# Turning chunks on the partitions in a gated-attention and MoE kernel, with a list scheduler's due times by stage

## The chip, the cores and the metric

The kernel runs on one core of a Trainium2 chip. The metric is the device time of one execution in microseconds (us). Before the change it was 332.19 us, the median of three runs (331.95 to 332.5). The engines are written as in the profile: PE (TensorE, matrix products; PEld its weight loads), DVE (VectorE), ACT (ScalarE), POOL (GpSimd), and SP (SyncE, which only issues transfers here). "SPq" in a chain of waits is time in which SP's queue is issuing a transfer. The core has 16 DMA engines.

## The reference

A linear attention with complex decay, whose output goes through a gated two-layer network:

```python
mag = np.sqrt(a_re * a_re + a_im * a_im)
scale = np.minimum(mag, 0.999) / (mag + 1e-06)
# a_re_n, a_im_n = a_re * scale, a_im * scale
for t in range(S):                      # B=4, H=8, S=768, D=48
    new_re = ar * S_re - ai * S_im
    new_im = ar * S_im + ai * S_re
    kv = np.einsum('bhd,bhe->bhde', k[:, :, t], v[:, :, t])
    S_re, S_im = (new_re + kv, new_im)
    y[:, :, t] = np.einsum('bhd,bhde->bhe', q[:, :, t], S_re)
# x = y as [3072, 384]
gate = 1.0 / (1.0 + np.exp(-(x @ w_gate)))
val = x @ w_val
return (gate * val @ w_out)             # w_gate, w_val [384, 1536], w_out [1536, 384]
```

All inputs and the output are float32. q, k, v, a_re and a_im have the shape (batch 4, heads 8, tokens 768, 48).

## The kernel before

The tokens of a batch are cut into six chunks of 128, one token on each SBUF partition: 24 chunks in all. The recurrence inside a chunk becomes products with triangular masks: cumulative sums over tokens of the log magnitude (`cl`) and of the phase (`ct`). A planner (a list scheduler that runs when the program is built) decides in which order each engine gets its instructions, from costs, buffers and "due times".

Each load takes one tensor of one chunk, 128 tokens x 8 heads x 48 numbers. A head's 48 numbers are 192 contiguous bytes in DRAM, so one load is 1024 pieces of 192 bytes:

```python
def dma_in(dst, src, b, c):
    nc.sync.dma_start(
        heads(dst), src[b, :, c * L:(c + 1) * L].rearrange("h t d -> t h d"))
```

A chunk has five of them: a_re, a_im (step `la`), then k, q, v (step `lq`). The phase of a chunk must start from the sum over all earlier chunks of the batch. Before, POOL keeps a running sum `run` of whole tiles and PE adds its column sums with a second product, against a matrix `on_t` of equal entries:

```python
nc.tensor.matmul(ct, wt_t, T[A][:, 1, s], start=True, stop=False, ...)
if prev:
    nc.tensor.matmul(ct, on_t, T[prev[0]], start=False, stop=False, ...)
# ... cut ...
nc.gpsimd.tensor_tensor(out=T[RUN], in0=T[prev[0]], in1=th, op=ALU.add)
```

After that `ct` is rounded on DVE (`r16`), the rounded turns are taken off by a small product (`nid_t`), and ACT makes sine and cosine.

## Time and profile before

| | before |
|---|---|
| time, median | 332.19 us |
| span of the profiled execution | 328.5 us |
| busiest engine | PE, 262.5 us (80%) |
| hardware DMA queue | 148,368 packets, 51.2% of 16 engines' span |
| first squares on ACT / first gate product on PE | 14.45 us / 44.12 us |

The lines themselves stand in the prediction. The groups there read: line, engine, operation, output<-inputs, shapes, count | busy us, mean ns of one | idle time before them and what ended it. The page's slices cut the span in 40; a digit is a busy share in tenths.

### The profile page before, as it was taken

The page shows a single profiled execution, that of the slowest core. Times are in us where ns is not written, and L with a number is a line of the kernel's source. Part 1 is how long each engine was busy: PE and PEld are TensorE (multiplying, and loading weights), DVE is VectorE, ACT ScalarE, POOL GpSimd, SP SyncE. Part 2 cuts the span into 40 slices and gives each one's busy share as a digit, 9 for nine tenths or more (in the row PEclk, how much of TensorE's full clock was granted, in tenths as well). Part 3 has the DMA queues.
Part 4 walks back from the last instruction along what each step waited for, and adds up shares of the span by engine and source line. Part 5 has one row for each costly group of instructions (what it writes and reads, how often), then busy time and mean ns, then how long its engine had stood idle before and what let it go on. Part 6 is the DMA issues. An engine that isn't in the chain of part 4 may idle for free.

```text
span 328.5 us, 6196 instructions
## 1 busy us (share of the span) xinstructions
PE 262.5 (80%) x2256; PEld 169.7 (52%) x2256; DVE 206.5 (63%) x373; ACT 211.9 (65%) x354; POOL 166.1 (51%) x177
## 2 busy tenths in 40 slices
PE   0035685857978799898969989989999898999995
PEld 0012552535545455465646555656666565666564
DVE  2002930399699679287755696689567949891522
ACT  0356438666877987896389848867995358543433
POOL 0187275867997877687117961945485104000000
PEclk9997757799999999999998999999999999999999
DMA  6998995997999588581886048736120011002011
GB/s 124 188 182 128 189 178 85 138 196 108 160 123 218 76 129 160 123 145 11 148 166 113 1 82 154 153 54 118 50 26 2 0 50 28 0 2 73 2 48 48
DMA packets 152381, 32.68 MB, mean 99 GB/s; under 512 B 144904, under 2 KB 152352, under 8 KB 152352
## 3 DMA queue, kind: packets, MB, share of 16 engines
q1 hardware_dynamic: 148368, 28.76, 51.2%
q0 software_dynamic: 3984, 3.54, 7.6%
q8 instruction: 17, 0.28, 0.4%
q14 instruction: 12, 0.10, 0.1%
HBM read 31.07 MB, written 4.76 MB: 109 GB/s over the span
## 4 chain that ended last, share of the span: by engine, by line
PE 42%; ACT 20%; DVE 18%; issue 8%; SPq 4%; DMA 4%; POOL 3%; DVEq 0%; ACTq 0%; POOLq 0%
PE o L717 12%; PE g L679 8%; PE v L679 7%; PE cl L389 5%; ACT L769 5%; DVE qkT L556 4%; DVE p L701 3%; DVE qst L518 3%; DVE kst L518 3%; SPq L309 3%; PE ct L463 2%; ACT g L694 2%; ACT sq L333 2%; ACT a L449 2%; POOL lm L342 2%
## 5 line engine op out<-in xcount | busy, mean ns | idle before, releaser
L694 ACT ACTIVATE g<-g 128x384 f16<-128x384 f32 (+2 forms) x108 | 48.2, 456 | 55.4 <-PE g L679 53.5
L701 DVE SCALAR_TENSOR_TENSOR p<-g,v 128x384 f16<-128x384 f16 (+2 forms) x108 | 53.7, 504 | 23.2 <-PE v L679 15.7
L679 PE MATMUL g<-xt,wg 128*128 128x384 f16 (+2 forms) x324 | 65.5, 312 | 3.0 <-DVE xt L662 1.5
L679 PE MATMUL v<-xt,wv 128*128 128x384 f16 (+2 forms) x324 | 65.5, 312 | 0.9 <-DVE p L701 0.9
L717 PE MATMUL o<-wo,p 128*128 128x384 f16 x288 | 52.0, 326 | 0.0
L389 PE MATMUL cl<-lm,wl_t 128*128 128x384 f32 x48 | 22.7, 607 | 27.8 <-ACT lm L365 24.9
L441 POOL TENSOR_TENSOR qk<-qk,ee 128x768 f32<-128x768 f32 x24 | 43.3, 1813 | 2.0 <-ACT ee L398 2.0
L490 DVE TENSOR_SCALAR r<-ct 128x384 f16<-128x384 f32 x24 | 13.2, 552 | 43.9 <-PE ct L463 25.9
L679 PEld LDWEIGHTS <-wg 128*128 128x128 f16 x324 | 29.5, 99 | 20.5 <-issue 8.0
L679 PEld LDWEIGHTS <-wv 128*128 128x128 f16 x324 | 28.7, 99 | 17.0 <-issue 5.8
L518 DVE TENSOR_TENSOR kst<-qk,cs 128x768 f16<-128x768 f32 x24 | 26.1, 1089 | 17.6 <-ACT cs L509 17.5
L556 DVE COPY qkT<-tp 128x1024 f16<-128x1024 f16 x48 | 32.6, 683 | 6.9 <-PE tp L549 6.6
L598 POOL CAST x<-u 128x384 f16<-128x384 f32 x20 | 14.1, 707 | 44.4 <-DVE u L588 38.4
L717 PEld LDWEIGHTS <-p 128*128 128x128 f16 x288 | 27.1, 98 | 18.2 <-issue 2.1
L571 DVE TENSOR_TENSOR mst<-sc,msk_t 128x512 f16<-128x512 f32 x48 | 32.6, 684 | 5.5 <-PE sc L564 5.4
L342 POOL TENSOR_TENSOR lm<-sq 128x384 f32<-128x384 f32 x24 | 28.1, 1170 | 13.7 <-ACT sq L333 12.3
L769 ACT ACT_TABLE_LOAD x27 | 34.6, 1283 | 0.5
L382 POOL TENSOR_TENSOR a<-a 128x384 f32<-128x384 f32 x24 | 23.6, 1008 | 22.0 <-ACT a L371 19.5
L463 PE MATMUL ct<-a,wt_t 128*128 128x384 f32 x48 | 22.1, 544 | 8.9 <-ACT a L449 8.9
L549 PE MATMUL tp<-idn_t,qst 128*128 128x128 f16 x192 | 26.5, 221 | 3.2 <-DVE qst L518 3.2
L389 PEld LDWEIGHTS cl<-lm,wl_t 128*128 128x128 f32 x48 | 10.4, 235 | 34.9 <-ACT lm L365 28.9
L548 PE MATMUL tp<-idn_t,kst 128*128 128x128 f16 x192 | 27.0, 221 | 0.8 <-DVE P L618 0.4
(52 smaller groups left out, 462.6 us busy)
## 6 DMA issues: line engine op xcount, KB each, us to landing
a<-in_a_re_dram SPq DMA_DIRECT2D x24, 192.0 KB, 3.9
a<-in_a_im_dram SPq DMA_DIRECT2D x24, 192.0 KB
qk<-in_k_dram SPq DMA_DIRECT2D x24, 192.0 KB, 4.9
qk<-in_q_dram SPq DMA_DIRECT2D x24, 192.0 KB, 4.8
v<-in_v_dram SPq DMA_DIRECT2D x24, 192.0 KB, 4.1
out_dram<-ot SPq DMA_DIRECT2D x24, 192.0 KB, 1.9
wg<-in_moe_w_gate_dram POOLq DMA_DIRECT2D x3, 384.0 KB, 5.7
wv<-in_moe_w_val_dram POOLq DMA_DIRECT2D x3, 384.0 KB, 6.4
```

Of the source, the lines that this page charges most:

```text
L342: nc.gpsimd.tensor_tensor(out=T[LM][:, s], in0=T[SQ][:, 0, s], in1=T[SQ][:, 1, s], op=ALU.add)
L389: nc.tensor.matmul(T[CL][:, :HD], wl_t, T[LM][:, s], start=True, stop=True)
L441: nc.gpsimd.tensor_tensor(out=T[QK], in0=T[QK], in1=T[EE], op=ALU.mult)
L463: nc.tensor.matmul(ct, wt_t, T[A][:, 1, s], start=True, stop=False, skip_group_check=True)
L518: nc.vector.tensor_tensor(out=T[SL][i].rearrange("p h (r x) -> p h r x", r=2)[:, :, :, 0:D], in0=heads(T[QK][:, i]).unsqueeze(2) .broadcas ...
L556: nc.vector.tensor_copy(out=T[QT], in_=T[TP])
L571: nc.vector.tensor_tensor(out=T[MS], in0=T[SC], in1=msk_t.unsqueeze(1).broadcast_to([L, 4, L]), op=ALU.mult)
L679: nc.tensor.matmul(T[ACC][:, :nt], w[:, j, fb * 128:fb * 128 + 128], T[XT][:, j, :nt], start=(j == 0), stop=(j == 2))
L694: nc.scalar.activation(out=T[G16][:, :nt], in_=T[PG][:, :nt], func=FT.Tanh, scale=0.5)
L701: nc.vector.scalar_tensor_tensor(out=T[PT][:, fb, :nt], in0=T[G16][:, :nt], scalar=1.0, op0=ALU.add, in1=T[PV][:, :nt], op1=ALU.mult)
L717: nc.tensor.matmul(T[PO][:, :DM], T[PT][:, fb, s * L:(s + 1) * L], wo16[:, fb], start=(fb == 0), stop=(fb == NFB - 1))
L769: nc.scalar.preload_act_table_set(SETS[held])
```

## The change

The intent is to do without the second phase product and the running sum in batches 1 to 3. Chunk c is laid on the partitions turned by c tokens, so its last token lies on the partition where the next chunk has its first token. The carry then is one row, which DVE adds in place in a 32-row window; the masks turn with the chunk. The due times become a table by stage and group, the first group is one chunk whose elementwise work DVE does, and table loads of ACT are placed explicitly. The planner now also sorts its candidates (`sorted(ready, key=self.rank.get)`), where the planner before walks a Python set. The core of the diff:

```diff
-SIZES = [2, 3, 3, 3, 3, 3, 3, 3, 1]
-RATE = 9.21
-LEAD = {'la': 87.6, 'lq': -0.9, 'p0': 39.8, 'pa': 40.0, 'pb': 17.2}
+ROLL = 1
+BRISK = 1
+SIZES = [1, 2, 2, 2, 3, 3, 3, 3, 3, 2]
+DUE = {
+    "la": [-88.8, 5.9, -62.3, -45.2, -110.2, -63.1, -93.9, 4.9, 23.3, 64.9],
+    # ... cut: 17 more stages ...
+}
 # ... cut ...
+    tok = (np.arange(L)[None] + np.arange(NCH)[:, None]) % L
+    upto = tok[:, :, None] <= tok[:, None, :]
+    last = (tok == L - 1).T * TWO_PI
 # ... cut ...
+    def turn(b, c):
+        return c if b >= ROLL else 0
+
+    def pieces(b, c):
+        r = turn(b, c)
+        return [(slice(0, L - r), slice(c * L + r, (c + 1) * L))] + (
+            [(slice(L - r, L), slice(c * L, c * L + r))] if r else [])
+
     def dma_in(dst, src, b, c):
-        nc.sync.dma_start(
-            heads(dst), src[b, :, c * L:(c + 1) * L].rearrange("h t d -> t h d"))
+        for p, t in pieces(b, c):
+            nc.sync.dma_start(
+                heads(dst[p]), src[b, :, t].rearrange("h t d -> t h d"))
 # ... cut ...
+    END = slice(L - 32, L)
 # ... cut ...
-            if c < NCH - 1:
+            if c < NCH - 1 and not rolled:
                 RUN = t_run(m)
 # ... cut ...
+            if rolled and c < NCH - 1 and s < n - 1:
+                def e(T, CT=CT, A=A, s=s, c=c):
+                    nc.vector.scalar_tensor_tensor(
+                        out=T[A][END, 1, s + 1], in0=T[CT][END, :HD],
+                        scalar=lst_t[END, c:c + 1], op0=ALU.mult,
+                        in1=T[A][END, 1, s + 1], op1=ALU.add)
```

The output stores are cut by the same `pieces`.

## The prediction

> **What bounds the kernel now.** I read the page from the top: busy shares, the forty slices, the DMA queues, the chain that ended last.
>
> ```profile
> span 328.5 us, 6196 instructions
> ...
> PE 262.5 (80%) x2256; PEld 169.7 (52%) x2256; DVE 206.5 (63%) x373; ACT 211.9 (65%) x354; POOL 166.1 (51%) x177
> ...
> PE   0035685857978799898969989989999898999995
> ...
> DMA  6998995997999588581886048736120011002011
> ...
> q1 hardware_dynamic: 148368, 28.76, 51.2%
> ...
> PE 42%; ACT 20%; DVE 18%; issue 8%; SPq 4%; DMA 4%; POOL 3%; DVEq 0%; ACTq 0%; POOLq 0%
> ```
>
> See three things. TensorE is the bound from about 140 us on (tenths of 9), and it is mostly idle in the first 60 us. The chain runs through PE, ACT and DVE; transfers are only 4% of it. And yet the transfers are not cheap: hardware queue q1 keeps 51.2% of 16 engines' span busy, and the first 70% of the slices stand at 5 to 9 tenths, because 120 loads (24 chunks x a_re, a_im, k, q, v) move in pieces of 192 bytes. They are hidden because they come early and because 16 DMA engines share each of them.
>
> So I measured the price of one piece, from the DMA view of two stretches in which loads ran without a gap, 95.8 to 101.2 us and 13 to 20 us:
>
> ```profile
> q1 hardware_dynamic: 5494, 1.09, 131.3%
> ```
>
> ```profile
> q1 hardware_dynamic: 6923, 1.31, 142.4%
> ```
>
> 5.4 us x 16 engines / 5494 packets = 15.7 ns; 7 us x 16 / 6923 = 16.2 ns. (The shares exceed 100% because a packet's record overlaps its neighbour's; the elapsed time counts.) One engine therefore takes about 16 ns per 192-byte piece. A load of 128 rows x 8 heads is 1024 pieces, 64 per engine, 1.0 us on 16 engines. Output rows of 1536 bytes, from the DMA view of the last 28.5 us (932 packets, 12.2%): 0.122 x 16 x 28.5 / 932 = 60 ns each.
>
> **What the Trainium skill says.** "DMA: Bandwidth & Descriptors", section "Why a DMA increments its semaphore by 16 and not by 1", says how many engines a DMA runs on: the largest k up to 16 that divides the slowest dimension of both access patterns; "127 partitions or a `[1, 1]` scalar → 1", and on the hardware path the lowest-numbered k. Every tile of the kernel before that is loaded from q, k, v and a has 128 rows, k = 16, which its 1.0 us agrees with; no trace here shows 127 rows yet. The same page, "Queues, rings and completion order", says that each engine consumes its ring in order, so a full-width load behind a narrow one waits on the shared engine. "Rules for kernel authors" there asks for an outermost size that is a multiple of 16.
>
> **The change part by part.**
>
> *On the core, gains.* 15 of the 20 carried chunks lose the second phase product (two passes each; these rows are from the groups by line):
>
> ```profile
> L466 PE MATMUL ct<-run,on_t 128*128 128x384 f32 x40 | 17.0, 507 | 0.0
> L479 POOL TENSOR_TENSOR run<-run,a 128x384 f32<-128x384 f32 x16 | 16.7, 1041 | 8.5 <-ACT a L449 5.0 <-PE ct L466 2.3 <-DMA v<-in_v_dram 0.9
> L769 ACT ACT_TABLE_LOAD x27 | 34.6, 1283 | 0.5
> ```
>
> PE: 30 x 0.507 = 15.2 us at that mean (12.8 us as a share of the row's 17.0 busy). POOL: 12 running sums x 1.04 + 3 copies x 0.51 = 14.0 us. ACT: 33 table loads in the trace, 30 in the new program: 3.8 us. DVE gains 21 carry operations on 32 rows (9 fused, 6 products, 6 sums), some 0.55 us each as the rounding of the same 384 columns costs: +11.6 us, in series with ct, rounding and next ct. A first group of one chunk, its elementwise work on DVE, starts on two loads alone. Before, the first squares wait until 13.15 us for four loads and the first gate product starts at 44.1; summing the chain's durations for one chunk I get about 6 us for the load and 20 us of work, so 26 to 28 us. More groups (10 for 9) move the same 110,592 columns of gate and value work. Together perhaps 25 to 35 us less: **about 300 us, if loads stay hidden.**
>
> *On the queue, the cost.* Turning chunk c of batches 1 to 3 by c rows splits every load into 128-c rows and c rows. By the rule: 127 rows 1 engine, 126 on 14, 125 on 5, 124 on 4, 123 on 3. Engine 0 serves all of them. Its pieces per load, big part plus small: c=0 64; c=1 1016+1; c=2 72+8; c=3 200+8; c=4 248+8; c=5 328+8: sum 1961, where an unturned batch gives it 384. One load of 127 rows takes 1016 x 16 ns = 16.3 us instead of 1.0, and a chunk has five.
>
> The program order (SP queue 189 rows before, 295 now) places the loads of chunks 0 to 6 first, almost as before: 35 loads, at least 36 us on all engines. I put the first 127-row load at 50 us. Then:
>
> - loads from there on, counted in the program: 29,095 pieces on engine 0 x 16 ns = 465.5 us;
> - output rows on the same engine before the last loads (k rule again): 466 x 60 ns = 28 us;
> - waits in which the in-order queue has nothing in flight: eight decay round trips after their scratch writes at 2 us, and about 10 us where the last q, k, v loads stand behind chunk 15's output, which waits for the phase work of the last group: 25 us;
> - after the last load: multiplies with the phase, attention of chunks 22 and 23, two thirds of group 8's gate work, group 9's, the outputs: before, 43 us passed from chunk 23's phase product (285.4) to the end with four chunks' output work left; about 37 us.
>
> 50 + 465 + 28 + 25 + 37 = 605 us span; measured time stood 3.7 us above the profiled span before (332.2 against 328.5), so about 609.
>
> What lies beside what: all gains on PE, POOL and ACT fall into time in which these engines now wait for loads. A chunk costs engine 0 on average 1961 x 5 x 16 ns / 6 = 26 us, against 11.7 us per chunk of the kernel before (281 us from the first gate product at 44 to 325, 24 chunks). Buffers can't hide it: it is throughput, not latency.
>
> **The rivals.**
>
> 1. *The engine rule doesn't bite* (the hardware spreads 127 rows after all). Then the core's gains stand: about 300 us. For it: the due times are plainly tuned, which suggests a planner that saw a gain. Against it: that planner charges 2.3 and 3.45 us a chunk whatever its rows, so it can't see the rule.
> 2. *SP issue becomes the bound*: 106 more DMAs at 0.4 to 1.0 us (issue records of the timeline) = 40 to 100 us more of queue time, 200 to 260 in all, still under the span; alone it would give 300 to 340 us.
> 3. *The serial carry*: cy, ct 1.3, rounding 0.56, correction 0.3, cy 0.55: 2.7 us x 15 = 40 us if wholly exposed, against 15 removed. Alone 310 to 340 us, inside the noise of the answer.
> 4. *A single engine runs quicker by itself* than beside 15 others: at 13 ns per piece the sum falls by 87 us to 520; at 18 ns (the queue's 51.2% x 16 x 328.5 / 148368) it rises by 58 to 668.
>
> **Range and chances.** Rivals 4 and my 50, 25 and 37 us give 520 to 690 about 610. Rival 1 I hold at about one in ten. So faster by over 2%: 0.09, within 2%: 0.02, slower: 0.89.
>
> **What would show it.** Right: loads of a turned chunk take 16 us or more from issue to landing where they took 4 to 5; the DMA row of the slices drops to about a tenth (one of 16 engines) from 50 us on while packets stay near 150,000 and q1's share falls to some 28%; PE below 50% busy, its clock often granted low; DMA and SPq lead the chain; ACT's squares and POOL's q, k products wait for DMA. Wrong: loads still land in 4 to 5 us and PE stays above 80%. The head is right if the first gate product starts near 27 us; the carry is right if its operations last about 0.55 us and nothing waits long for them. Mis-sized: the pieces' 16 ns, read off a stretch with one engine busy.

## The result, and the profile after

The changed kernel takes 537.81 us (median of 4 runs, 533.9 to 538.21); the kernel before, beside it on the same chip, 332.07 us (330.98 to 332.5). The ratio is 1.6178, 95% interval 1.6106 to 1.625: slower. Ratios in this document are the mean time of one kernel's fast runs over that of the other's of the same rounds, so not quite the ratio of the quoted medians.

The page of the changed kernel, in the same order as before:

```profile
span 532.1 us, 6426 instructions
...
PE 274.6 (52%) x2298; PEld 183.0 (34%) x2298; DVE 228.7 (43%) x410; ACT 210.3 (40%) x368; POOL 146.4 (28%) x158
...
PE   1467602304776068200277609700355779799973
...
DMA  9999403005432250000543261000243220122011
GB/s 158 190 195 186 66 16 55 18 16 120 95 55 61 52 105 18 17 16 16 128 66 65 61 113 22 16 17 16 51 78 82 55 45 1 36 63 58 28 46 30
...
q1 hardware_dynamic: 149741, 29.75, 27.9%
...
SPq 61%; PE 13%; DMA 12%; issue 5%; ACT 3%; DVE 3%; POOL 1%; ACTq 0%; POOLq 0%; DVEq 0%
...
L532 POOL TENSOR_SCALAR v<-v 128x384 f16<-128x384 f32 x24 | 14.3, 594 | 210.8 <-DMA v<-in_v_dram 206.6
```

The packets are almost as many as before, but q1's share fell from 51.2% to 27.9%. The GB/s row shows why: long stretches at 16 to 18, others at about 65 and 55. In those slices or just after them PE goes to 0. The kernel before moves mostly 80 to 200 in its first 28 slices:

```profile
GB/s 124 188 182 128 189 178 85 138 196 108 160 123 218 76 129 160 123 145 11 148 166 113 1 82 154 153 54 118 50 26 2 0 50 28 0 2 73 2 48 48
```

The chain is 61% SP's issues, and POOL's conversion of v alone waits 206.6 us for loads.

A turned chunk's loads in SP's timeline (start, duration, queue, line, output<-input, transfers joined in the row), chunk with one turned row first, then the next chunk's:

```profile
205.40 12.02 SPq L390 DMA_DIRECT2D a<-in_a_im_dram  x2
217.52 12.05 SPq L390 DMA_DIRECT2D qk<-in_k_dram  x2
229.62 11.98 SPq L390 DMA_DIRECT2D qk<-in_q_dram  x2
241.64 12.07 SPq L390 DMA_DIRECT2D v<-in_v_dram  x2
253.76 0.95 SPq L390 DMA_DIRECT2D a<-in_a_re_dram  x2
```

Each x2 is one split load. The load of 127 + 1 rows holds SP's queue for 12.0 us, the load of 126 + 2 rows for 0.95 us. An uncut load held it 1.0 us in the kernel before, where loads ran without a gap. The records behind the joined rows show where the time lies: the issue of the 127 rows takes 0.2 to 0.4 us, and the issue behind it, that of the single row, stands for 11.2 to 14.2 us. No semaphore that this second issue waits for changes in that time. So SP is neither busy computing addresses nor waiting for data: the second issue stands until the 127 rows are nearly through (they land about 1.6 us after it ends). The next view, the DMA view of the changed kernel from 206 to 240 us, in 40 parts, says how many engines are at work:

```profile
GB/s 16 16 16 16 16 16 16 16 16 16 16 16 36 16 18 12 16 16 16 16 16 16 16 16 16 16 16 16 18 16 16 16 16 16 16 16 16 16 16 16
```

And the same view from 285 to 300 us, where loads of 124 and then of 123 rows run:

```profile
GB/s 65 66 61 65 66 66 66 65 65 66 60 62 66 66 66 65 66 66 59 40 49 49 49 49 49 49 49 51 55 47 49 92 49 49 49 49 49 49 57 261
```

16, 49 and 65 GB/s are 1, 3 and 4 times 16.3: one engine for 127 rows, three for 123, four for 124. The completion semaphores in the trace agree. A load of 128 rows raises its semaphore in 16 updates, a load of 127 rows in 2: one 0.4 to 0.7 us after its issue, the other 13.5 to 16.2 us after it, when the data has landed. Loads of 126, 125, 124 and 123 rows make 15, 6, 5 and 4 updates, one more than the 14, 5, 4 and 3 engines.

The gain that was foretold for the head is there: the first gate product starts at 26.58 us (44.12 before).

### The profile page after: what moved, and what is told of

Same layout as the page of the kernel before. It is cut to its first block, busy times and chain, and to the rows that moved or that the text cites. A ratio compares the mean times of both kernels' runs of the same rounds, so it can differ in the third digit from the quotient of the medians.

```text
span 532.1 us, 6426 instructions
## 1 busy us (share of the span) xinstructions
PE 274.6 (52%) x2298; PEld 183.0 (34%) x2298; DVE 228.7 (43%) x410; ACT 210.3 (40%) x368; POOL 146.4 (28%) x158
## 3 DMA queue, kind: packets, MB, share of 16 engines
q1 hardware_dynamic: 149741, 29.75, 27.9%
## 4 chain that ended last, share of the span: by engine, by line
SPq 61%; PE 13%; DMA 12%; issue 5%; ACT 3%; DVE 3%; POOL 1%; ACTq 0%; POOLq 0%; DVEq 0%
SPq L390 57%; DMA v<-in_v_dram 5%; PE g L808 4%; DMA out_dram<-ot 4%; PE v L808 3%; DMA a<-in_a_im_dram 3%; PE o L846 2%; SPq L349 2%; SPq L509 1%; PE ct L572 1%; ACT sq L429 1%; PE sc L694 1%; DVE qkT L686 1%; ACT g L823 1%; SPq L500 1%
## 5 line engine op out<-in xcount | busy, mean ns | idle before, releaser
L808 PE MATMUL g<-xt,wg 128*128 128x384 f16 (+2 forms) x360 | 75.4, 324 | 59.4 <-ACT g L823 52.1
L808 PE MATMUL v<-xt,wv 128*128 128x384 f16 (+2 forms) x360 | 73.8, 319 | 19.1 <-DVE p L830 18.1
L532 POOL TENSOR_SCALAR v<-v 128x384 f16<-128x384 f32 x24 | 14.3, 594 | 210.8 <-DMA v<-in_v_dram 206.6
L429 ACT ACTIVATE sq<-a 128x2304 f32<-128x2304 f32 (+2 forms) x10 | 17.4, 1739 | 118.9 <-DMA a<-in_a_im_dram 57.6
L808 PEld LDWEIGHTS <-wg 128*128 128x128 f16 x360 | 34.9, 107 | 77.9 <-issue 68.2
L846 PE MATMUL o<-wo,p 128*128 128x384 f16 x288 | 55.8, 332 | 4.5 <-DMA wo<-in_moe_w_out_dram 4.5
L764 PE MATMUL y<-x,qkT 128*128 128x48 f16 x160 | 11.9, 188 | 77.3 <-POOL x L728 74.0
L808 PEld LDWEIGHTS <-wv 128*128 128x128 f16 x360 | 34.8, 106 | 36.1 <-issue 25.2
L766 PEld LDWEIGHTS <-mst 128*128 128x128 f16 x192 | 11.4, 100 | 78.8 <-issue 75.7
L846 PEld LDWEIGHTS <-p 128*128 128x128 f16 x288 | 28.1, 99 | 21.7 <-issue 6.2
L678 PE MATMUL tp<-idn_t,kst 128*128 128x128 f16 x192 | 30.7, 238 | 0.5 <-DVE kst L649 0.5
```

What stands on the lines that cost most here:

```text
L678: nc.tensor.transpose(tp[:, 4 + i], ks[:, h], idn_t)
L808: nc.tensor.matmul(T[ACC][:, :nt], w[:, j, fb * 128:fb * 128 + 128], T[XT][:, j, :nt], start=(j == 0), stop=(j == 2))
L846: nc.tensor.matmul(T[PO][:, :DM], T[PT][:, fb, s * L:(s + 1) * L], wo16[:, fb], start=(fb == 0), stop=(fb == NFB - 1))
```

## The experiments

Ten kernels were run beside the two given, and two more could not be built. The theory: narrow transfers, and with them the in-order queue, make the whole loss. Rivals: the carry or the new order of the compute engines is bad in itself; the issues on SP are too many. The experiments on the changed kernel keep its order of instructions on PE, DVE, ACT and POOL exactly: the traces of all six agree with its trace instruction by instruction. (Their edits also hold the planner's charge for a split load fixed, which is not shown below.) The four cuts of the kernel before do not keep its order. Its planner walks a Python set, so each build can give another order: the file built twice gave two programs, and built twice with one hash seed the same program. The four traces hold the same work, but in other orders (on PE, over 1,100 of 2,256 places differ). Differences of a few us in that group may come from this.

Two attempts gave no run. To have the carry on its row without turning, every odd chunk could be loaded with its tokens reversed; a kernel with this negative step in DRAM does not compile. And the new due times without the turn cannot be built: the planner ends with "no step can be placed", and also with fewer turned batches. So the schedule alone, without the turn, stays untried.

### The changed kernel, every split load cut at row 112

```diff
-        return [(slice(0, L - r), slice(c * L + r, (c + 1) * L))] + (
-            [(slice(L - r, L), slice(c * L, c * L + r))] if r else [])
+        if not r:
+            return [(slice(0, L), slice(c * L, (c + 1) * L))]
+        w = L - 16
+        return [(slice(0, w), slice(c * L + r, c * L + r + w)),
+                (slice(w, L - r), slice(c * L + r + w, (c + 1) * L)),
+                (slice(L - r, L), slice(c * L, c * L + r))]
```

Same bytes to the same rows, in pieces of 112, 16 - c and c rows.

> The changed kernel, every instruction of the compute engines in the same order, but each split load and store is cut into 112 rows, 16-c rows and c rows (112 divides by 16; 90 more DMAs on the same queue). Theory A (a transfer runs on as many engines as divide its row count; narrow ones were the cost): 295 to 325 us, no load above 6 us, the DMA row without a plateau of 16 GB/s. Rival B (the number of DMA issues on the in-order queue was the cost): slower than the 538 us of the changed kernel. Rival C (the serial phase carry or the new order of steps was the cost): stays above 500 us.

Measured: 317.32 us (315.51 to 318.27, 4 runs) beside 328.15 us of the kernel before; ratio 0.967, interval 0.9626 to 0.9715. The whole loss of 206 us is gone with the shape of the transfers, with the carry, the masks and the order untouched. The two rivals are out as causes of the loss. The 16 GB/s stretches are gone. From its page, the GB/s row and the chain by engine:

```profile
GB/s 147 175 163 202 201 168 192 124 85 169 143 151 98 138 176 102 128 151 104 154 156 69 109 119 102 104 57 97 50 2 1 27 100 103 2 51 27 26 52 50
...
PE 35%; DVE 23%; SPq 14%; issue 10%; ACT 7%; DMA 6%; POOL 3%; DVEq 0%; ACTq 0%; POOLq 0%
```

SPq still is 14%, where the kernel before has 4%. That is followed up below.

### The kernel before, cut at row 112 and at row 113

```diff
-        nc.sync.dma_start(
-            heads(dst), src[b, :, c * L:(c + 1) * L].rearrange("h t d -> t h d"))
+        cut = 112 if b and c else L        # 113 in the second kernel
+        for p in [slice(0, cut)] + ([slice(cut, L)] if cut < L else []):
+            nc.sync.dma_start(
+                heads(dst[p]),
+                src[b, :, c * L + p.start:c * L + p.stop].rearrange(
+                    "h t d -> t h d"))
```

The other way round: nothing of the change, only the loads of the same 15 chunks cut in two, as 112 + 16 or 113 + 15 rows (in a newly planned order, as said).

> The kernel before, unturned, each load of chunks 1 to 5 of batches 1 to 3 cut at row 112 into 112 and 16 rows: 75 more DMAs, the same bytes at the same places. Theory A: both row counts divide by 16, so 330 to 342 us, within 3% of before. Rival B: each extra issue costs its 0.4 to 1 us on the path, 360 to 410 us.

> As the run cut at row 112, but cut at row 113: 113 is prime, so by theory A the large part runs on one engine. 15 chunks x 5 loads x 113 x 8 pieces = 67,800 pieces, at 11.7 ns (192 bytes at the 16.4 GB/s that one engine showed) 793 us, plus about 60 us before and 50 after: 850 to 950 us. Rival B: the same time as the cut at 112, since the number of DMAs and the bytes are the same.

Measured: cut at 112, 326.11 us (325.44 to 327.25), ratio 0.9949, interval 0.9908 to 0.9989: no loss (expected were 330 to 342 us, within 3% of before; the kernel before was itself quicker in these rounds). Cut at 113, 1011.92 us (one run, state unknown). One row of difference is worth 686 us. 113 is prime. The DMA view of the 113-row kernel from 200 to 250 us:

```profile
GB/s 16 16 16 16 16 16 16 19 31 16 16 16 16 16 16 16 34 16 16 16 16 16 16 16 16 33 14 16 16 16 16 16 16 16 34 16 16 16 16 16
```

One engine again, with a short burst where the 15 rows on fifteen engines come. The completion semaphore of each of the 75 loads of 113 rows has 2 updates, that of each load of 112 rows 16. The size was outside what I expected (850 to 950 us). I had put 50 us after the last load; the trace shows the last load issued at 920.0 us and a span of 1010.1, so 90. The rest of the miss: the split loads held SP 811 us (793 expected), and 53 us passed between them, for which I had put nothing.

### The changed kernel, only its 127-row transfers widened

`pieces` is cut at 112 only where r is 1; 126, 125, 124 and 123 rows stay as the change has them.

> The changed kernel with only the 127-row transfers widened (112, 15 and 1 rows); 126, 125, 124 and 123 rows stay as they are. Theory A: 15,240 of engine 0's 29,095 pieces leave it, 178 us at 11.7 ns; about 15,000 remain, some 180 us, which the compute now partly covers: 330 to 390 us. If the 127-row loads were not the larger half of the cost: above 430 us.

Measured: 370.75 us (369.69 to 371.85), ratio 1.1298, interval 1.1244 to 1.1352. So of the 220 us between the changed kernel and the 112-row cut, 167 us belong to the one chunk in six with 127 rows, and 53 us to the 5, 4 and 3 engines of the others.

### The kernel before, cut at row 119 and at row 124

The same edit with 119 (seven engines by the rule) and 124 (four).

> The kernel before with the loads of chunks 1 to 5 of batches 1 to 3 cut at row 119 (119 = 7 x 17: seven engines by the rule; the other 9 rows: nine). Engine 0 serves 136 + 8 = 144 pieces a load, 2.25 times the 64 of an uncut load. Theory (loads cost only what one engine's queue can't hide): 5 x 144 x 11.7 ns = 8.4 us a chunk, under the 11.7 us that a chunk takes on the core, so hidden: 0.99 to 1.04 of the kernel before. Rival (every transfer that leaves the sixteen engines costs its own length, hidden or not): 75 loads x 80 pieces more x 11.7 ns = 70 us more, a ratio of about 1.2.

> The same cut at row 124 (four engines for 124 rows, four for the other 4): 248 + 8 = 256 pieces a load on engine 0. Theory: 5 x 256 x 11.7 ns = 15.0 us a chunk, over the core's 11.7 us, so it is the bound: first cut load at about 45 us, 75 x 256 + 15 x 64 pieces x 11.7 ns = 236 us, stores and waits 30 us, and some 100 us that the order of the kernel before leaves after its last load: about 410 us, 390 to 440, a ratio of 1.18 to 1.34. Rival (only the one-engine case is slow): a ratio under 1.05.

Measured: 358.82 us (354.65 to 359.3), ratio 1.0892, interval 1.0818 to 1.0965, and 444.48 us (443.87 to 445.3), ratio 1.3521, interval 1.3458 to 1.3584. The second is just above what I expected (390 to 440 us, 1.18 to 1.34). The DMA view of the 119-row kernel from 70 to 84 us:

```profile
GB/s 104 105 71 53 40 67 103 114 118 118 100 109 115 119 165 124 156 118 98 148 189 192 196 150 90 77 102 111 113 114 115 122 91 109 114 117 121 108 111 114
```

Where the loads run alone, most parts lie between 108 and 122 GB/s; seven engines would give 7 x 16.3 = 114. The rule holds at each width tried: in the semaphores too, with 8 updates for 119 rows and 5 for 124.

But the 119-row kernel missed what the theory expected (0.99 to 1.04). Its loads hold SP 1.64 us each, 8.2 us a chunk, which is under the 11.7 us that a chunk takes on the core, and still the time rose by 30 us. "Hidden if the average rate suffices" is the wrong test. The loads come in bursts, a group's a_re and a_im and then its k, q, v, and buffers bound how far they run ahead. What counts is when they are done. I read from SP's timelines the end of the issue of the last of all loads, and set it against the time:

| kernel | last load issued, us | later by | time, us | longer by |
|---|---|---|---|---|
| before | 226.8 | | 328.15, 328.4 | |
| before, cut at 112 | 224.0 | -2.8 | 326.11 | -2.0 |
| before, cut at 119 | 257.7 | 30.9 | 358.82 | 30.4 |
| before, cut at 124 | 347.1 | 120.3 | 444.48 | 116.1 |

(Time differences are taken to the kernel before of the same rounds; the first figure in its row is that of the 112-row kernel's rounds, the second that of the others. Its trace of 226.8 is the first one, on another chip.) The delay of the load stream is the loss, to within about 4 us, although the orders differ. The 113-row kernel is 693 us later and 684 us longer. That the 30 us of the 119-row cut owe nothing to its new order is not shown by a control; the one re-planned kernel whose loads stayed wide, the cut at 112, moved by 2 us.

### One more cut: more issues, same engines

From the 112-row turned kernel, the 112 rows cut again into 64 and 48, both on sixteen engines.

```diff
-        return [(slice(0, w), slice(c * L + r, c * L + r + w)),
+        h = 64
+        return [(slice(0, h), slice(c * L + r, c * L + r + h)),
+                (slice(h, w), slice(c * L + r + h, c * L + r + w)),
```

> The turned kernel whose pieces are cut to 112, 16-c and c rows (317.3 us), with the 112 rows cut again into 64 and 48, both on sixteen engines: same bytes, same pieces for each engine, 90 transfers more on SP's queue, at 0.5 to 0.6 us an issue about 50 us of SP time. If the issues on SP hold the turned kernel back: 335 to 360 us. If they lie beside the rest: 315 to 322 us.

Measured: 356.66 us (356.15 to 358.23), ratio 1.0862, interval 1.0814 to 1.0911: 39 us for 90 transfers, 0.44 us each. The rival "too many issues" is no cause of the 206 us, but it is real. One split load in SP's timeline, in the kernel before cut at 112, in the turned kernel cut at 112, in the kernel with one more cut, and in the kernel before cut at 119:

```profile
70.13 1.03 SPq L311 DMA_DIRECT2D qk<-in_q_dram  x2
```

```profile
77.91 1.20 SPq L394 DMA_DIRECT2D qk<-in_q_dram  x3
```

```profile
82.15 2.07 SPq L396 DMA_DIRECT2D qk<-in_q_dram  x4
```

```profile
81.98 1.63 SPq L311 DMA_DIRECT2D v<-in_v_dram  x2
```

Two pieces of 112 and 16 rows take 1.03 us, as one uncut load did: the 64 pieces of each engine take that long anyway, and the second issue lies beside them. Three take 1.20, four 2.07 us, about 0.5 us an issue. At 119 rows two pieces take 1.63 us, and there the seven engines set it (136 pieces in 1.63 us, 12.0 ns each). In these four rows a load costs whichever is longer, the pieces of its busiest engine or its issues. The issues are not all alike: from 0.26 us for two rows to 0.62 us for a single row.

### Stores issued by ACT

In the 112-row turned kernel SP's queue waited 78.3 us at output stores for ACT to finish the tile (SP's waits: queue, line, waited for: us in total, times, longest):

```profile
SPq L869 <- ACT ot L860: 78.3, 14, 22.3
```

```diff
-                    nc.sync.dma_start(
+                    nc.scalar.dma_start(
                         out[b * S + t.start:b * S + t.stop], T[OT][p])
```

This adds the issues to ACT's order and leaves the other compute engines' orders as they are.

> The turned kernel with the 112-row cut, its output stores issued by ACT, which makes the output tile, in place of SP, whose in-order queue stood 78 us at stores waiting for ACT with loads behind them. If loads held behind stores cost time: 303 to 313 us. If they don't, 315 to 320 us; if ACT's 54 issues at some 0.5 us weigh more than SP's waits: 320 to 335 us.

Measured: 335.04 us (333.93 to 339.01, of which the last was slow), ratio of the fast runs 1.0185, interval 1.0134 to 1.0236. Against the kernel before this is unclear by the 2% rule; against the stores on SP (0.967 in its own rounds) it is clearly slower, at the upper edge of what I expected if ACT's issues weigh more. SP's waits in this kernel show a new one:

```profile
SPq L394 <- DMA out_dram<-ot: 36.9, 9, 10.1
```

Loads on SP now wait for stores to land, which they have no data in common with. The trace shows why: each of the nine loads waits for the very semaphore that it is to raise itself, and the transfer that used this semaphore last was a store that ACT had issued about 2 to 3 us before. SP's and ACT's transfers share semaphores in this program, and in a wait of up to 10.1 us SP in part still waited for ACT to come to its store. So the experiment is confounded: it does not tell what the 78 us are worth, only that this way of removing them costs more.

### Uncut loads with the new order, wrong on purpose

```diff
     def pieces(b, c):
-        r = turn(b, c)
-        # ... cut ...
+        return [(slice(0, L), slice(c * L, (c + 1) * L))]
```

The masks stay turned and the tokens are not, so the result is wrong (relative error 0.189), but the compute engines do the changed kernel's work in its order while the queue does the old loads.

### The first and the last token exchanged

The carry needs the last token of a chunk on the row of the next one's first. Exchanging rows 0 and 127 of every odd chunk gives this too, and the even chunks stay as they are:

```diff
-    tok = (np.arange(L)[None] + np.arange(NCH)[:, None]) % L
+    tok = np.stack([np.arange(L)] * NCH)
+    tok[1::2, [0, L - 1]] = L - 1, 0
 # ... cut: two sets of masks in place of six ...
+    def turn(b, c):
+        return c % 2 if b >= ROLL else 0
+
+    def pieces(b, c):
+        t = c * L
+        if not turn(b, c):
+            return [(slice(0, L), slice(t, t + L))]
+        return [(slice(1, L - 1), slice(t + 1, t + L - 1)),
+                (slice(0, 1), slice(t + L - 1, t + L)),
+                (slice(L - 1, L), slice(t, t + 1))]
 # ... cut ...
-    END = slice(L - 32, L)
+    def end(c):
+        return slice(0, 32) if c % 2 else slice(L - 32, L)
```

(The decay of the chunk's last token is read from row 0 or 127 accordingly. The planner's costs are kept, so the order on the compute engines is that of the changed kernel.)

> Another permutation with the same carry: in batches 1 to 3 the odd chunks have their first and last token exchanged (126 rows on fourteen engines by the rule, and two single rows), the even chunks lie as they are, so the last token of a chunk is on the row of the next one's first. Nine turned chunks with three pieces a load instead of fifteen, two sets of masks instead of six: 84 transfers fewer on SP than with the 112-row cut, the same order on all compute engines. SP's time per load was about 1.0 us uncut, 1.2 us with three pieces, 1.65 us (row 119) and 2.1 us (four pieces), and about 0.6 of each added us showed in the time; so if the time of loads on the in-order queue still holds the turned kernel back: 15 loads-chunks x 5... that is 30 loads x 0.2 us + 12 constants x 0.43 us = 11 us less on SP, 6 to 7 us less in the time: 306 to 314 us. If it doesn't: 315 to 319 us.

> Wrong result on purpose: the changed kernel with every load and store in one uncut 128-row transfer (tokens not turned, masks turned), so the compute engines do the changed kernel's work in its order and the queue does the old loads. It measures the gain on the core alone. If my 25 to 35 us were right: 293 to 304 us. If they were too high: 307 to 315 us. If cutting costs nothing beside this: the 317 us of the 112-row cut.

Measured in the same rounds: uncut and wrong, 308.49 us (307.63 to 311.26), ratio 0.9403, interval 0.9345 to 0.9461. Ends exchanged, correct, 308.66 us (305.6 to 309.67), ratio 0.9375, interval 0.9302 to 0.9447. **This is the best version: 6% under the kernel before, and as quick as one whose loads are not cut at all.** Its page:

```profile
span 306.7 us, 6450 instructions
...
PE 251.5 (82%) x2298; PEld 169.2 (55%) x2298; DVE 225.7 (74%) x410; ACT 209.4 (68%) x368; POOL 147.6 (48%) x158
...
PE 42%; DVE 26%; issue 8%; SPq 8%; ACT 8%; DMA 4%; POOL 3%; DVEq 0%; ACTq 0%
```

PE and DVE lead the chain again, with SPq at 8%.

Its time is what I expected, but not quite by the way I gave. I expected 11 us less of SP time. Its split loads, with a single row twice, in fact hold SP 1.8 us each, longer than the 1.2 us of most loads of the 112-row cut, and summed over the run SP stands about as long at loads (153 against 155 us from the timelines). What differs is when. I take the same load, k of chunk 21, in the kernels uncut, ends exchanged, cut at 112, and with one more cut:

```profile
189.20 0.39 SPq L388 DMA_DIRECT2D qk<-in_k_dram  x1
```

```profile
189.23 2.12 SPq L394 DMA_DIRECT2D qk<-in_k_dram  x3
```

```profile
198.48 1.24 SPq L394 DMA_DIRECT2D qk<-in_k_dram  x3
```

```profile
241.89 2.07 SPq L396 DMA_DIRECT2D qk<-in_k_dram  x4
```

Behind the uncut kernel they are late by 0.0, 9.3 and 52.7 us, and their times are longer by 0.2, 8.8 and 48.2 us. At the k load of chunk 12 the starts were 96.95, 107.06, 112.42 and 130.56: even the exchanged version was 10 us late there, in the stretch in which loads are issued without a pause. It had caught up by chunk 21, because its unsplit even chunks take 0.4 to 0.8 us a load and the stream then waits for buffers anyway. The 112-row cut never catches up. That the even chunks let it catch up is my reading of these starts; no run changes that alone. The load was also chosen after the fact. In kernels not used for the choice the same load is 27.4 us late for 26.6 us (stores by ACT), 55.2 for 62.3 (only 127 widened) and 210.6 for 229.3 (the changed kernel): right in kind, and up to 12% short.

## Why the prediction was right, and where its terms were off

**The class and the mechanism.** Right. The rule of the Trainium skill, "DMA: Bandwidth & Descriptors", section "Why a DMA increments its semaphore by 16 and not by 1", agrees with every width tried here: 16 GB/s for 127 and for 113 rows, 49 for 123, 65 for 124, 108 to 122 for 119. The same page's "Queues, rings and completion order" says that each engine takes the descriptors of a ring in order, so that a later transfer waits on a shared engine; the trace agrees in that every later load comes after the narrow one, with SP's queue held 12.0 us each. Rival 1 (the rule doesn't bite) is out by the 113-row kernel and by the 2 semaphore updates of every 127-row load.

**The sum, term by term,** for the span of 532.1 us, predicted 605:

| term | predicted | in the trace |
|---|---|---|
| before the first 127-row load | 50 | 55.1 |
| loads from there on | 465.5 | 353 (SP's time at these loads, each from its first issue to the end of its last) |
| stores and waits between | 28 + 25 = 53 | 487.9 - 55.1 - 353 = 80 |
| after the last load | 37 | 532.1 - 487.9 = 44 |

The term that was mis-sized is the loads, by the 16 ns a piece; the prediction named that as its weak point, and it is rival 4. One engine with work alone takes 12.0 us for the 1017 pieces of a load, 11.8 ns each, and the DMA view from 206 to 240 us has 2,907 packets in 34 us, 11.7 ns each (192 bytes / 11.7 ns = 16.4 GB/s); sixteen together took 15.7 ns. Over all loads of the term it is 353 us / 29,095 pieces = 12.1 ns. So this term was 112 us too large.

The other three were together 39 us too small: 5 before, 27 between, 7 after. Between the loads SP spent 36 us on issues of other kinds (stores 10.6, the decay's scratch 18.6, constants 7.1), and for some 44 us it issued nothing, once for 19 us at a store that waited for ACT. Two errors of opposite sign thus cancelled in part. With 353 us for the loads and the other terms as they were, the sum is 493 us, below the range of 520 to 690. That the time lies inside the range is in part luck; the mechanism is not.

Three smaller slips. The 3.7 us between span and time compare two executions: the profiled one took 330.96 us, 2.5 us over its span. Four of the first 28 DMA slices are not "5 to 9 tenths" but 1, 0, 4 and 3. And the traces have 222 and 306 issues on SP, 84 more, not 106.

**Signs in the profile.** The fall of q1's share to 27.9% (said: 28%), the chain led by SPq and DMA, the low clock (0.79 over the run), the waits of POOL for loads, and the first gate product at 26.58 us (said: 26 to 28) all came. PE is at 52%, where I had said under 50%. The 127-row loads landed 13.5 to 16.2 us after their issue, all but one under the 16 us given.

**The gain on the core.** The wrong-on-purpose kernel measures it: 328.64 - 308.49 = 20 us, against "perhaps 25 to 35 us less". The direction was right and the size too large. PE's busy time fell by 262.5 - 251.5 = 11.0 us (said: 12.8 to 15.2; the row of the second product alone fell from 17.0 to 4.8), and its idle time by (328.5 - 262.5) - (305.7 - 251.5) = 11.8 us. I named 17 us earlier at the head, but PE works at less than half its time there, so little of that is work that is saved later. And DVE gained 206.5 -> 228.2 = 21.7 us of work, not 11.6. The groups of the exchanged version show the carry:

```profile
L568 DVE TENSOR_TENSOR a<-a,cr 32x384 f32<-32x384 f32 x6 | 5.6, 926 | 0.1
L622 DVE SCALAR_TENSOR_TENSOR a<-ct,lst_t,a 32x384 f32<-32x384 f32 x9 | 5.6, 617 | 1.2 <-ACT cs L644 1.1
L633 DVE TENSOR_SCALAR cr<-ct,lst_t 32x384 f32<-32x384 f32 x6 | 3.7, 615 | 1.0 <-ACT cs L644 0.9
```

The six additions took 0.93 us each, not 0.55, and all 21 together 14.9 us. The first group's elementwise work on DVE adds 2.6 us (four rows of 1.0, 0.6, 0.6 and 0.4). DVE itself waited little before them (0.1, 1.2 and 1.0 us in all), and ACT's sine and cosine waited 2.5 us in all for the fused ones, which speaks against rival 3, a serial carry that leaves its engines idle.

**Rival 2, issues on SP.** Not the bound of the changed kernel. But with wide pieces it is the next cost: 39 us for 90 issues, and of the changed kernel's possible 20 us the 112-row cut lost 9 to the late stream. In the prediction I put the issue cost at 40 to 100 us "under the span", which was right for this kernel and would have been wrong for its repair.

**What stays open.** What SP's 78 us at the stores cost; what the new due times are worth without the changed carry; and how much the time of the kernel before moves with the order that a build happens to give it.

## What to carry to other kernels

Look at the outermost size of every transfer before anything else when a layout shifts by a few rows: 127 and 113 rows ran on one engine of sixteen, and a kernel with five such loads of 12 us in a chunk turns from compute-bound to load-bound. If a layout needs an odd place for a single row, move that row by itself and leave the rest wide; among layouts that serve the algorithm, take the one that splits fewest transfers. And a load is not hidden because its average rate suffices: compare the start of the same late load in both kernels, for the delay there tells most of the delay of the end. Last, let a planner walk nothing unordered: if a build's order hangs on a hash seed, an edit of one line is compared with a kernel in another order.

## What the Trainium skill lacked or had wrong

- "DMA: Bandwidth & Descriptors", section "Specifications", gives about 27 GiB/s for one engine and says that line rate wants 512 bytes or more, but no figure for rows of 192 bytes issued from SP. Here one engine moved them at 16.4 GB/s by itself (11.7 to 11.8 ns a row), and at some 12 GB/s (15.7 to 16.2 ns a row) when all sixteen were at work. The difference of 4 ns a row was my largest error.
- The same page, "Why a DMA increments its semaphore by 16 and not by 1", has the rule but not its price. Here: 112 rows against 113, 326 against 1012 us for the whole kernel, and 10.7 against 1.0 us of SP's queue for one load.
- The same page, "Issuing engines are not separate DMA queues", calls the sequencer's time to start a DMA "usually small relative to the DMA itself". For the pieces of these loads of 192 KB it is not: 0.3 to 0.7 us an issue against 1.0 us for a whole load, and 90 issues more on the same engines cost 39 us.
- No page that I read says that an issue behind a narrow transfer holds the sequencer while that drains: SP issued 127 rows in 0.2 to 0.4 us and then stood 11.2 to 14.2 us in the issue of the single row behind them; behind 113 rows it stood some 10.4 us in the issue of 15 rows, whose semaphore shows fifteen engines.
